# Induced attention and two MLPs: chunk 1's softmax steps, a PSUM bank, a sign vector and four dummy products are moved or added

## The chip, the cores and the metric

The kernel runs on one core of a Trainium2 chip. Its time is the device time of one execution in microseconds (us); the time before is the median of three runs, 992.58 us (991.95 to 992.87). The engines are named as the profile names them: PE is TensorE's products, PEld its weight loads, DVE is VectorE, ACT is ScalarE, POOL is GpSimd, SP is SyncE, which here issues transfers. A q behind a name is the engine's instruction queue.

## The reference

There are 12480 tokens x of 128 channels and 32 inducing vectors. Then come three stages, one after the other, all in float32 (the MLP weights arrive as float64):

```python
def mab(q, kv):
    s = scale * (q @ kv.transpose(0, 2, 1))
    s = s - s.max(-1, keepdims=True)
    a = np.exp(s)
    a /= a.sum(-1, keepdims=True) + 1e-09
    return a @ kv
h = mab(I, x)              # 32 rows
x = mab(x, h)              # 12480 rows
h = x @ w_in;  x = (h * np.cos(h)) @ w_out             # 128 -> 2048 -> 128
h = x @ w_in2; out = (h / (1 + np.exp(-h))) @ w_out2   # 128 -> 2048 -> 128
```

## The kernel before, in words

**Prologue (lines 284 to 688, up to about 50 us).** The tokens are loaded and transposed, and the first attention is done over all of them. Its result is folded into the first MLP's input weights (`project`, 628 to 648). `project_hi` on ScalarE and `project_lo` on VectorE write the stacked weights `hw[0..3]`; `project_lo` reads the sign vector `s_w`, which lies in the prologue's pool `pp` (line 294). The softmax of chunk 0 is done here too, and `spread(1)` issues the sixteen transfers that put block 1's weights of attention into the stack buffer `stk`.

**Main loop (`main`, 716 to 1005).** Tokens go through in 7 chunks (lines 70 to 74): chunk 0 has 8 tiles, chunk 6 has 10, the others 16. Each chunk makes 4 blocks of up to 512 columns, chunk 0 makes 2, so there are 26 blocks. A block takes 8 steps, one for each pair of hidden tiles of 128, so there are 208 steps (NU), and the second MLP runs L2 = 11 steps behind the first. The code emits the instructions of a step in a fixed order by hand (969 to 1005), and each engine takes its own in that order:

- `mlp1_in(s)` (727): two products into `h1` (two buffers in PSUM); `mlp1_act` (742): Sin on ScalarE, the multiply on VectorE, the rounded copy `hi`; `mlp1_rest` (788): the remainder `lo` on VectorE; `mlp1_out` (823): six products into `acc1`, in steps below WHOLE1 = 12 two whole float32 products instead. At the end of a block `y_split` (833) makes `yhi` on ScalarE and `ylo` on VectorE from `acc1`.
- `mlp2_in` (844): six products into `h2` (one buffer); `mlp2_act` (862): Silu and `hi` on ScalarE, `lo` on GpSimd; `mlp2_out` (887): six products into `acc2` two steps later (below WHOLE2 = 8 two whole ones); `store` (897) at the end of a block: a transpose on VectorE and transfers.
- `held_back` (963 to 967) tells where in a step `mlp2_in` and Silu stand: 0 is ahead of `mlp2_out`, 1 behind it, 2 behind `mlp1_out` too.
- `joined`, `worded` and `splitting` (704 to 708) tell in which early steps the remaining weight pieces are converted: `narrow_body` and `narrow_tail` on ScalarE, `narrow_sign` and the first half of `narrow_join` on VectorE, its sum on GpSimd, followed by the transfer of a further piece (`fetch`) on SP's queue; `split` is a cast on ScalarE and a subtraction on GpSimd. Step 4 begins with the body of the piece that step 0 fetched.

**Softmax of the later chunks.** `soften` (928) does one of six things: take (scores by products into the bank of `h2`, transposed by VectorE at line 220), centre (a maximum on VectorE, a subtraction on GpSimd), exp (ScalarE, with a table load before and after), norm (230: sum, add and reciprocal on VectorE, the multiply on GpSimd), turn (237: a transpose on VectorE), split (240: a cast on ScalarE, a subtraction on GpSimd). `chunk_step` (944) looks up which thing a chunk does in which step: `second` (710) for chunk 1, by step; `later` (711) for the others, counted from 24 steps ahead of the chunk's first block, which is a multiple of 8. `attend` (949) calls them, exp early in a step, the rest at its end behind the weight split. `fill` (956) issues a block's transfers into the stack; block 2, the first of chunk 1, is needed by the products of step 16 and was filled at the end of step 15.

**PSUM.** It has eight banks: h1 takes 0 to 3, h2 takes 4 and 5, acc1 is 6 and acc2 is 7. Projections 2 and 3 lie in banks 4 and 5 in the prologue, projections 0 and 1 in 6 and 7.

Of the kernel before, what the change touches and what calls it, by code (L numbers as in the profile page):

```python
# [9 lines left out]
F32 = mybir.dt.float32  # L10
# [11 lines left out]
def tile_induced_attention_then_two_mlps(  # L22
# [31 lines left out]
    nc = tc.nc  # L54
# [4 lines left out]
    P, G, Q = 128, 4, 32  # L59
    NF = FF // P  # L60
    NJ = NF // 2
# [19 lines left out]
    persist = ctx.enter_context(tc.tile_pool(name="persist", bufs=1))  # L81

    half_pi = persist.tile([P, 1], F32, name="half_pi")
    quarter = persist.tile([P, 1], F32, name="quarter")
    hT4 = persist.tile([C, G, M], F32, name="hT4")

    held = persist.tile([P, G * W], F32, name="held")
# [4 lines left out]
    hw = [persist.tile([P, FF // 4], F32R, name=f"hw{i}") for i in range(4)]  # L92
# [152 lines left out]
    blocks, first_of = [], []  # L245
# [11 lines left out]
    stacks = {}  # L257

    def places(b):

        at, out = 0, []
        for g, t, m in blocks[b][1]:
            n = width((t, m), g)
            out.append((g, t, m, at, n))
            at += n
        return out

    def cols(b):
        return sum(n for *_, n in places(b))

    def spread(b, st):
        t0 = st["span"][0]
        stack = stk[:, b % 2, :]
        for g, t, m, at, n in places(b):
            a = (t - t0) * Q
            for r in range(G):
                src = st["hi"].bitcast(F32) if r < 2 else st["lo"]
                nc.sync.dma_start(
                    out=stack[r * Q : (r + 1) * Q, at : at + n].bitcast(F32),
                    in_=src[g * Q : (g + 1) * Q, a : a + n],  # L280
                )
        stacks[b] = stack

    with ExitStack() as pro:
        pp = pro.enter_context(tc.tile_pool(name="pp", bufs=1))
# [5 lines left out]

        fold = pp.tile([P, M], F32, name="fold")
        fold4 = pp.tile([P, G, M], F32, name="fold4")
        s_w = pp.tile([P, 1], F32, name="s_w")
        ones = pp.tile([P, 1], F32, name="ones")
        warm = pp.tile([P, 1], F32, name="warm")
        indT = pp.tile([C, M], F32, name="indT")
# [25 lines left out]
        spin = ps_h.tile([P, 512], F32, tag="hp", name="spin")[:, 0:P]  # L323
# [220 lines left out]
        for i in range(end):  # L544

            k = i - 2 if i < 2 + NP else None
# [51 lines left out]
            lhsT=fold4.rearrange("p g m -> p (g m)"),  # L598
            rhs=zacc[end % 2],
            start=True,  # L600
            stop=True,
# [3 lines left out]
        spin = ps_h.tile([P, 512], F32, tag="hp", name="spin")[:, 0:P]  # L605
# [65 lines left out]
        for i, v in enumerate((hi0, lo0)):  # L671
            for g, t, m, at, n in places(0):
                nc.tensor.matmul(
                    top[:, at : at + n],
                    lhsT=pick[:, g, 2 - 2 * i : 6 - 2 * i, :].rearrange("p r m -> p (r m)"),
                    rhs=v[:, t * Q : t * Q + n],
                    start=(i == 0 and g == 0),
                    stop=(i == 1 and g == G - 1),
# [13 lines left out]
    psh = ctx.enter_context(tc.tile_pool(name="psh", bufs=1, space=PSUM, reuse_waits="tile"))  # L692
    psa = ctx.enter_context(tc.tile_pool(name="psa", bufs=1, space=PSUM, reuse_waits="tile"))
# [6 lines left out]
    LEAD, FILL = 24, 8  # L700
# [6 lines left out]
    splitting.update(zip((13, 15, 11, 12), range(NP, 2 * NP)))  # L707
    splitting.update(zip((17, 18, 19, 20), range(3 * NP, 4 * NP)))

    second = {3: "take", 5: "centre", 12: "exp", 13: "norm", 14: "turn", 14.5: "split"}  # L710
    later = {0: "take", 2: "centre", 5: "exp", 7: "norm", 10: "turn", 11: "split"}

    def d1(u):
        return 2 if u < WHOLE1 else 1
# [1 line left out]
    def main(general):  # L716
# [3 lines left out]
        acc1, acc2 = {}, {}  # L720
# [6 lines left out]
        def mlp1_in(u):  # L727
            b, j = divmod(u, NJ)
            n = cols(b)
            ps = psh.tile([P, 2, 512], F32, tag="h1", name="h1", bufs=2)  # L730
            for a in range(2):
                f = 2 * j + a
                nc.tensor.matmul(  # L733
                    ps[:, a, 0:n],
                    lhsT=hw[f // 4][:, f % 4 * P : (f % 4 + 1) * P],
                    rhs=stacks[b][:, 0:n],
                    start=True,
                    stop=True,
                )
            hid1[u] = ps  # L740

        def mlp1_act(u):
            b, j = divmod(u, NJ)
            n = cols(b)
            h = hid1.pop(u)[:, :, 0:n]
            whole = u < WHOLE1
            c = u1.tile(
                [P, 2, W],
                F32,
                tag=("hi1", "lo1")[u % 2] if whole else "c",  # L750
                name="c",
                bufs=2 if whole else 1,
            )
            cs = c[:, :, 0:n]
            if general:
                turns = cs.bitcast(I32)
                nc.scalar.activation(turns, h, AF.Identity, bias=quarter, scale=0.5 / PI)
                nc.vector.scalar_tensor_tensor(
                    out=cs,
                    in0=turns,  # L760
                    scalar=2.0 * PI,
                    in1=h,
                    op0=ALU.mult,
                    op1=ALU.subtract,
                )
                nc.scalar.activation(cs, cs, AF.Sin, bias=half_pi, scale=-1.0)
            else:
                nc.scalar.activation(cs, h, AF.Sin, bias=half_pi, scale=1.0)  # L768
            if u in worded:
                narrow_body(worded[u])  # L770
                narrow_tail(worded[u])

            nc.vector.tensor_tensor(cs if whole else h, h, cs, ALU.mult)  # L773
            if whole:
                g1[u] = c
                join(u)
                return
            hi = u1.tile([P, 2, W], F32R, tag="hi1", name="hi1")
            nc.vector.tensor_copy(hi[:, :, 0:n], h)  # L779
            join(u)  # L780
            g1[u] = (hi, h)
# [31 lines left out]
        def down_whole(acc, w, c, j, n):  # L813
            for a in range(2):
                nc.tensor.matmul(  # L815
                    acc[:, 0:n],
                    lhsT=w[:, 2 * j + a, :],
                    rhs=c[:, a, 0:n],
                    start=(j == 0 and a == 0),
                    stop=(j == NJ - 1 and a == 1),  # L820
                )

        def mlp1_out(u):
            b, j = divmod(u, NJ)
            n = cols(b)
            if j == 0:
                acc1[b] = psa.tile([P, 512], F32, tag="acc1", name="acc1")
            if u < WHOLE1:
                down_whole(acc1[b], wf1, g1.pop(u), j, n)
            else:  # L830
                down(acc1[b], wo1, g1.pop(u), j, n)
# [112 lines left out]
        def chunk_step(k, s):  # L944
            if k == 1:
                return second.get(s)
            return later.get(s + LEAD - first_of[k] * NJ)

        def attend(s, early):
            for k in range(1, NK):  # L950
                for at in (s, s + 0.5):
                    what = chunk_step(k, at)
                    if what and (what == "exp") == early:
                        soften(chunk_soft[k], what)

        def fill(s):
            for b in range(2, NB):
                if s == b * NJ - (1 if b == 2 else 5 if blocks[b][0] == 1 else FILL):
                    spread(b, chunk_soft[blocks[b][0]])

        held_back = {}
        for k in range(1, NK):
            for s in range(NU):
                if chunk_step(k, s) == "exp":
                    held_back[s + 1], held_back[s + 2] = 2, 1

        for s in range(NU + L2 + D2 + 1):
            if s < NU:  # L970
                mlp1_in(s)
            v = s - L2
            place = held_back.get(s, 0)
            into = [False] * 3
            if 0 <= v < NU:
                into[place] = True
            if into[0]:
                mlp2_in(v)
            if s < L2:
                out1(s)  # L980
            if s < NU:
                mlp1_act(s)
            attend(s, True)
            if into[0]:
                mlp2_act(v)
            v = s - L2 - D2
            if 0 <= v < NU:
                mlp2_out(v)
                if v % NJ == NJ - 1:
                    store(v // NJ)  # L990
            v = s - L2
            if into[1]:
                mlp2_in(v)
                mlp2_act(v)
            if s < NU:
                mlp1_rest(s)
            if s >= L2:
                out1(s)
            if into[2]:
                mlp2_in(v)  # L1000
                mlp2_act(v)
            if s in splitting:
                split(splitting[s])
            attend(s, False)
            fill(s)

    hot = nc.values_load(flag[0:1, 0:1], min_val=0, max_val=1)
    saved = dict(stacks)
    ahead = len(order) - len(pieces)
    with tc.If(hot == 0) as arm:  # L1010
        main(False)
    stacks = saved
    with arm.Else():
        main(True)
# [34 lines left out]
```

## Time and profile before

| | us |
|---|---|
| median of three runs | 992.58 |
| the profiled execution's own time | 992.66 |
| its span, first to last instruction | 990.8 |
| prologue, up to the first product of the main loop | 48.8 |
| steps 0 to 16, up to the products of step 17 | 48.8 to 114.6 |
| a plain step later on | 4.59 |

How to read it: the rows come from one execution, so lengths are compared within it, and a gain is made against its 992.66 us. A product's own duration overlaps with the next one's, so the pace is read from starts. An idle stretch in brackets is the engine's idle time just before that row, with what ended it. PEclk is the granted share of TensorE's full clock of 2.4 GHz; its other level is 1.2 GHz, which is 0.5.

### The profile page before, as it was taken

Reading aid. Unit: us, or ns where it says so; the run is one execution under the profiler, and the core shown is the slowest. Engines: PE = TensorE matmul, PEld = TensorE weight load, DVE = VectorE, ACT = ScalarE, POOL = GpSimd, SP = SyncE. Lnnn points to the kernel's source line nnn. Section 1 sums busy time; section 2 is a strip of 40 time slices with the busy share of each in tenths; the row PEclk is TensorE's granted clock in tenths of the full one; section 3 lists DMA queues with packets and bytes.
Section 4 is the critical chain, followed back from the end, with each engine's and each line's share of the span. In section 5 each row is a group of like instructions: output and inputs, shape, how many; then the busy total and the mean of one; then the engine's idle time right before and its main releaser. Section 6 shows DMA issues by size and latency. Waiting matters only on the chain.

```text
span 990.8 us, 12394 instructions
## 1 busy us (share of the span) xinstructions
PE 966.6 (98%) x4659; PEld 773.5 (78%) x4659; DVE 786.5 (79%) x818; ACT 703.1 (71%) x764; POOL 507.9 (51%) x265
## 2 busy tenths in 40 slices
PE   8889899999999999999999999999999999999997
PEld 6545577788887788887788887788887888889996
DVE  4877778888888888888888888888888888867871
ACT  5777466876776777776877676867766867777774
POOL 1244255555545554555554555555555555465555
PEclk9989899999999999999999999999999999999999
DMA  9331010010110100110100100100100100000000
GB/s 350 105 118 40 22 22 1 11 30 3 22 22 1 22 16 7 22 19 3 23 12 10 22 16 6 22 12 11 22 13 9 22 11 8 18 17 13 13 8 16
DMA packets 65229, 28.21 MB, mean 28 GB/s; under 512 B 54312, under 2 KB 59784, under 8 KB 65160
## 3 DMA queue, kind: packets, MB, share of 16 engines
q1 hardware_dynamic: 64504, 27.24, 11.1%
q8 instruction: 38, 0.62, 0.3%
q14 instruction: 31, 0.25, 0.1%
q10 hardware_dynamic: 656, 0.09, 0.1%
HBM read 14.79 MB, written 6.39 MB: 21 GB/s over the span
## 4 chain that ended last, share of the span: by engine, by line
PE 80%; DVE 9%; ACT 3%; issue 2%; POOL 1%; DMA 0%; SPq 0%; ACTq 0%; POOLq 0%
PE acc L805 46%; PE h L853 24%; PE h L733 8%; DVE lo L795 2%; DVE h L773 2%; DVE hi L779 2%; ACT c L768 2%; PE acc L815 1%; ACT s L868 1%; DVE ylo L839 1%; POOL tail L152 0%; DVE sm L232 0%; DVE sm L233 0%; DVE s L220 0%; DVE sign L144 0%
## 5 line engine op out<-in xcount | busy, mean ns | idle before, releaser
L877 POOL TENSOR_TENSOR lo<-s,hi 128x1024 fp32r<-128x1024 f32 (+2 forms) x197 | 448.0, 2274 | 387.0 <-ACT hi L876 355.8
L805 PE MATMUL acc<-hi,wo 128*128 128x512 f32 (+2 forms) x1584 | 409.7, 380 | 0.9 <-DVE ylo L839 0.7
L773 DVE TENSOR_TENSOR h<-h,c 128x1024 f32<-128x1024 f32 (+2 forms) x196 | 227.5, 1161 | 136.6 <-ACT c L768 136.2
L805 PEld LDWEIGHTS acc<-hi,wo 128*128 128x128 f32 x1584 | 288.2, 188 | 60.2 <-DVE ylo L839 3.0
L768 ACT ACTIVATE c<-h,half_pi 128x1024 f32<-128x1024 f32 (+2 forms) x208 | 221.2, 1064 | 157.6 <-PE h L733 155.7
L868 ACT ACTIVATE s<-h 128x1024 f32<-128x1024 f32 (+2 forms) x208 | 202.5, 974 | 73.1 <-PE h L853 69.8
L853 PE MATMUL h<-yhi,wi 128*128 128x512 f32 (+2 forms) x832 | 248.8, 381 | 2.9 <-DVE s L220 2.2
L805 PE MATMUL acc<-lo,wo 128*128 128x512 f32 (+2 forms) x792 | 235.3, 378 | 0.1
L779 DVE CAST hi<-h 128x1024 fp32r<-128x1024 f32 (+2 forms) x196 | 226.1, 1154 | 6.8
L795 DVE TENSOR_TENSOR lo<-h,hi 128x1024 fp32r<-128x1024 f32 (+2 forms) x196 | 225.1, 1149 | 5.8
L876 ACT CAST hi<-s 128x1024 fp32r<-128x1024 f32 (+2 forms) x197 | 196.8, 999 | 6.3
L853 PEld LDWEIGHTS h<-yhi,wi 128*128 128x128 f32 x832 | 152.3, 188 | 36.4 <-DVE s L220 4.4
L805 PEld LDWEIGHTS acc<-lo,wo 128*128 128x128 f32 x792 | 145.8, 188 | 29.6 <-POOL lo L882 0.4
L853 PE MATMUL h<-ylo,wi 128*128 128x512 f32 (+2 forms) x416 | 157.4, 378 | 0.0
L733 PE MATMUL h<-stk,hw 128*128 128x512 f32 (+2 forms) x416 | 128.2, 389 | 8.0 <-DMA stk<-at 4.0
L733 PEld LDWEIGHTS h<-stk,hw 128*128 128x128 f32 x416 | 76.4, 190 | 33.7 <-issue 12.1
L853 PEld LDWEIGHTS h<-ylo,wi 128*128 128x128 f32 x416 | 78.4, 188 | 14.6
L815 PE MATMUL acc<-c,wf 128*128 128x512 f32 x48 | 24.3, 632 | 1.4 <-DVE ylo L839 1.4
L838 ACT CAST yhi<-acc 128x512 fp32r<-128x512 f32 (+2 forms) x26 | 14.6, 560 | 15.1 <-PE acc L805 14.9
L900 DVE STREAM_TRANSPOSE o<-acc 128x512 f32<-128x512 f32 (+2 forms) x26 | 17.5, 674 | 7.6 <-PE acc L805 7.6
L839 DVE TENSOR_TENSOR ylo<-acc,yhi 128x512 fp32r<-128x512 f32 (+2 forms) x26 | 16.9, 649 | 7.7 <-ACT yhi L838 7.7
L773 DVE TENSOR_TENSOR c<-h,c 128x1024 f32<-128x1024 f32 x12 | 14.7, 1222 | 7.3 <-ACT c L768 5.9
(141 smaller groups left out, 330.3 us busy)
## 6 DMA issues: line engine op xcount, KB each, us to landing
out_dram<-o SPq DMA_DIRECT2D x80, 64.0 KB, 2.0
x_sb<-in_x_dram SPq DMA_DIRECT2D x8, 512.0 KB, 9.9
raw<-in_moe_w_in_dram SPq DMA_DIRECT2D x8, 512.0 KB, 5.4
raw<-in_moe_w_out_dram SPq DMA_DIRECT2D x8, 512.0 KB, 3.8
stk<-ahi SPq DMA_DIRECT2D x40, 64.0 KB, 2.0
stk<-at SPq DMA_DIRECT2D x40, 64.0 KB, 2.0
x_sb<-in_x_dram SPq DMA_DIRECT2D x3, 256.0 KB, 3.3
x_sb<-in_x_dram SPq DMA_DIRECT2D x2, 320.0 KB
```

The source lines that it names most:

```text
L733: nc.tensor.matmul(ps[:, a, 0:n], lhsT=hw[f // 4][:, f % 4 * P : (f % 4 + 1) * P], rhs=stacks[b][:, 0:n], start=True, stop=True,)
L768: nc.scalar.activation(cs, h, AF.Sin, bias=half_pi, scale=1.0)
L773: nc.vector.tensor_tensor(cs if whole else h, h, cs, ALU.mult)
L779: nc.vector.tensor_copy(hi[:, :, 0:n], h)
L795: nc.vector.tensor_tensor(lo[:, :, 0:n], h, hi[:, :, 0:n].bitcast(F32), ALU.subtract)
L805: nc.tensor.matmul(acc[:, 0:n], lhsT=wt[:, 2 * j + a, :], rhs=gt[:, a, 0:n], start=(j == 0 and p == 0 and a == 0), stop=(j == NJ - 1 and p ...
L815: nc.tensor.matmul(acc[:, 0:n], lhsT=w[:, 2 * j + a, :], rhs=c[:, a, 0:n], start=(j == 0 and a == 0), stop=(j == NJ - 1 and a == 1),)
L839: nc.vector.tensor_tensor(lo[:, 0:n], y[:, 0:n], hi[:, 0:n].bitcast(F32), ALU.subtract)
L853: nc.tensor.matmul(ps[:, a, 0:n], lhsT=wt[:, fs], rhs=yt[:, 0:n], start=(p == 0), stop=(p == 2),)
L868: nc.scalar.activation(sv, hid2.pop(u)[:, :, 0:n], AF.Silu)
L876: nc.scalar.copy(hv, sv)
L877: nc.gpsimd.tensor_tensor(lv, sv, hv.bitcast(F32), ALU.subtract)
```

## The change

`s_w` is put into the lasting pool, behind `half_pi` and `quarter`, so it outlives the prologue. Chunk 1 does norm and turn at the end of step 12 (as 12.25 and 12.5) and split at the end of step 13; they stood in steps 13, 14 and 14. The transfers of block 2 are issued in step 13 instead of 15. The other chunks do exp and norm one step sooner. `acc1` of block 0 takes the bank of `acc2`. In the step after a take, `mlp2_in` and Silu stand behind `mlp2_out`. In step 1, four products with 512 columns that nobody reads are issued into the bank of `h2`.

```diff
     quarter = persist.tile([P, 1], F32, name="quarter")
+    s_w = persist.tile([P, 1], F32, name="s_w")
...
-        s_w = pp.tile([P, 1], F32, name="s_w")
...
-    second = {3: "take", 5: "centre", 12: "exp", 13: "norm", 14: "turn", 14.5: "split"}
-    later = {0: "take", 2: "centre", 5: "exp", 7: "norm", 10: "turn", 11: "split"}
+    second = {3: "take", 5: "centre", 12: "exp", 12.25: "norm", 12.5: "turn", 13: "split"}
+    later = {0: "take", 2: "centre", 4: "exp", 6: "norm", 10: "turn", 11: "split"}
...
+        def keep_awake(n):
+
+            ps = psh.tile([P, 2, 512], F32, tag="h2", name="spin")
+            for _ in range(n):
+                nc.tensor.matmul(
+                    ps[:, 0, :], lhsT=hw[0][:, 0:P], rhs=stacks[0], start=True, stop=True
+                )
...
-                acc1[b] = psa.tile([P, 512], F32, tag="acc1", name="acc1")
+                acc1[b] = psa.tile([P, 512], F32, tag="acc1" if b else "acc2", name="acc1")
...
-                for at in (s, s + 0.5):
+                for at in (s, s + 0.25, s + 0.5):
...
-                if s == b * NJ - (1 if b == 2 else 5 if blocks[b][0] == 1 else FILL):
+                if s == b * NJ - (3 if b == 2 else 5 if blocks[b][0] == 1 else FILL):
...
                 if chunk_step(k, s) == "exp":
                     held_back[s + 1], held_back[s + 2] = 2, 1
+                elif chunk_step(k, s) == "take":
+                    held_back[s + 1] = 1
...
                 mlp1_in(s)
+            if s == 1:
+                keep_awake(4)
```

## Rows read from the trace of the kernel before

**Rows 1.** The page, part 1: busy time, share of the span, instructions.
```profile
PE 966.6 (98%) x4659; PEld 773.5 (78%) x4659; DVE 786.5 (79%) x818; ACT 703.1 (71%) x764; POOL 507.9 (51%) x265
```
**Rows 2.** Timeline of PE, 48 to 110: start, length, work, [idle before].
```profile
53.16 1.22 PE L733 MATMUL h<-stk,hw 128*128 128x512 f32 x2 [3.13 <-DVE c L773]
...
76.33 1.98 PE L815 MATMUL acc<-c,wf 128*128 128x512 f32 x4 [1.35 <-DVE ylo L839]
...
106.94 1.19 PE L733 MATMUL h<-stk,hw 128*128 128x512 f32 x2 [4.04 <-DMA stk<-at]
```
**Rows 3.** Windows of early stages: stretch, length, busy by engine, PEclk, DMA share, GB/s.
```profile
53.20:57.70 4.50, 4.50 (x7) 2.24 (x8) 3.57 (x6) 3.46 (x5) 2.05 (x2) 0.52 0.10 26
...
75.00:90.00 15.00, 13.13 (x39) 7.20 (x40) 10.01 (x11) 13.35 (x18) 6.36 (x5) 1.00 0.19 50
...
107.00:113.00 6.00, 6.00 (x13) 3.76 (x13) 5.17 (x5) 3.28 (x4) 2.52 (x2) 0.57 0.18 44
```
**Rows 4.** Windows of single steps: after take, plain, behind norm and the y split.
```profile
303.20:308.62 5.42, 5.00 (x25) 3.78 (x21) 4.53 (x5) 3.20 (x3) 1.31 (x2) 1.00 0.02 3
308.62:313.21 4.59, 4.59 (x21) 3.75 (x20) 2.96 (x4) 3.19 (x3) 2.40 (x2) 1.00 0.00 0
340.80:345.84 5.04, 4.86 (x22) 3.68 (x20) 4.94 (x6) 3.68 (x4) 3.45 (x3) 1.00 0.00 0
```
**Rows 5.** Table of waits: who waited for whom, us, times, longest.
```profile
PEld h L853 <- DVE s L220: 4.4, 5, 1.0
...
PEld acc L805 <- DVE ylo L839: 3.0, 5, 0.6
```
**Rows 6.** Timeline of all engines, 42 to 66.
```profile
47.74 2.70 DVE L641 SCALAR_TENSOR_TENSOR hw<-hw,s_w,hwps 128x512 fp32r<-128x512 f32 x4
...
48.83 1.20 PE L733 MATMUL h<-stk,hw 128*128 128x512 f32 x4 [0.74 <-ACT stk L680]
...
50.68 1.11 ACT L768 ACTIVATE c<-h,half_pi 128x1024 f32<-128x1024 f32 x1 [1.91 <-DVE hw L641]
...
58.40 1.30 SPq L128 DMA_DIRECT2D raw<-in_moe_w_in_dram  x3
...
62.64 0.67 ACT L135 ACTIVATE body<-raw 128x512 f32<-128x512 f32 x1
```
**Rows 7.** The page, part 6: issues, KB each, median us to landing.
```profile
raw<-in_moe_w_out_dram SPq DMA_DIRECT2D x8, 512.0 KB, 3.8
```
**Rows 8.** Timeline of DVE, 84 to 110 and 321 to 323.
```profile
91.32 1.23 DVE L773 TENSOR_TENSOR h<-h,c 128x1024 f32<-128x1024 f32 x1 [3.18 <-ACT c L768]
...
94.79 1.22 DVE L795 TENSOR_TENSOR lo<-h,hi 128x1024 fp32r<-128x1024 f32 x1
...
96.64 0.98 DVE L233 TENSOR_SCALAR sm<-sm 128x16 f32<-128x16 f32 x1
...
101.46 0.70 DVE L238 STREAM_TRANSPOSE at<-s 128x512 f32<-128x512 f32 x1
...
322.02 0.71 DVE L900 STREAM_TRANSPOSE o<-acc 128x512 f32<-128x512 f32 x1
```
**Rows 9.** Timeline of ACT, 84 to 110.
```profile
102.20 0.62 ACT L241 CAST ahi<-at 128x512 fp32r<-128x512 f32 x1 [4.62 <-DVE at L238]
```
**Rows 10.** Timeline of POOL, 84 to 108.
```profile
90.35 1.29 POOL L179 TENSOR_TENSOR wo<-wf,wo 128x512 fp32r<-128x512 f32 x1 [3.44 <-ACT wo L178]
...
97.98 1.05 POOL L235 TENSOR_TENSOR s<-s,sm 128x512 f32<-128x512 f32 x1 [0.40 <-DVE sm L234]
...
102.89 1.26 POOL L242 TENSOR_TENSOR at<-at,ahi 128x512 f32<-128x512 f32 x1 [3.86 <-ACT ahi L241]
```
**Rows 11.** The chain that ended last, 84 to 125: start, length, work.
```profile
104.73 2.07 DMA stk<-at
...
114.61 0.47 PE h L733 x2
...
119.59 0.47 PE h L733 x2
```

## The prediction

> **What bounds the kernel now.** I read the page's engine shares first, then the timeline and the windows of the stages in which TensorE idles, then the length of single steps and the table of waits. TensorE is busy 98% of the span [rows 1], so only time in which it stands, or runs at the lower of its two clock levels (1.2 and 2.4 GHz), can be won. Before 115 us chains of the other engines bind: the products stand 3.13, 1.35 and 4.04 us [rows 2], and the granted clock is 0.52 after the first stand and 0.57 after the last [rows 3]. After 115 us a plain step takes 4.59 us, and two steps of a chunk are longer for a wait: the one after "take" (5.42) and the one behind "norm" and the y split (5.04) [rows 4]. There are five such chunks [rows 5].
>
> The profiled execution took 992.66 us, 0.08 above the median of 992.58. The sum is made against 992.66.
>
> **The first wait (s_w, dummy products, bank).** Sin of step 0 starts at 50.68, held by project_lo, which ends at 47.74 + 2.70 = 50.44 [rows 6]. The tile c of step 0 lies over the prologue's pool, and what project_lo reads there is s_w. Once s_w has its own place, Sin(0) waits for its products alone; they start at 48.83 [rows 6], so by about 49.6 they are done, 1.1 us sooner. The multiply behind it, and with it the products that start at 53.16 [rows 2], then come near 52.0. Should another tile hold Sin(0) as well, this gain is nil, and the sum hardly moves, as follows.
>
> The four dummy products write the bank pair of h2, where projections 2 and 3 are read until 50.44. So they run from 50.5, at 4.59 / 20 = 0.23 each [rows 4] or, at the low clock, twice that, and end between 51.4 and 52.3: 0 to 0.3 us at the third step's products. Whatever clock they keep, Sin(4), at 61.6 now, comes sooner by 1 to 2.9 us. There the gain stops: the next piece on ScalarE is "body", now at 62.64, which reads a weight piece issued at 58.40 [rows 6], behind sixteen stack transfers on SP's queue, and that issue doesn't move. A piece of these weights takes a median of 3.8 us to land where it goes alone [rows 7], so body starts at 62.2 at the earliest. Between 0 and 0.44; I take **0.4**, since what precedes body gains more than that in every case.
>
> From body to step 12 a loop sets the time: Sin, multiply, sign, GpSimd's join, ScalarE's split, next Sin. The stand of 1.35 on ylo [rows 2] is what the other bank for block 0's acc1 removes. The loop doesn't pass through it; the products would stand for the next multiply instead. Taken at **0**, bounds 0 and 1.35.
>
> **Second chunk.** Now the turn comes at 101.46, in step 14, behind that step's VectorE pieces and step 13's norm [rows 8]. ScalarE stands 4.62 us for it, up to 102.20, in front of Sin(15) [rows 9]. Then follow GpSimd's subtraction (to 104.15 [rows 10]), the transfers (to 106.80 [rows 11]) and the products of step 16 at 106.94 [rows 2]. The change moves norm (three small VectorE pieces, one GpSimd multiply) and turn to the end of step 12, the split and block 2's four transfers to the end of step 13; SP's queue has nothing else in those steps.
>
> - The exponential keeps its place on ScalarE, ahead of the cast that GpSimd waits for at 90.35 [rows 10]. VectorE is idle from 88.14 (91.32 less 3.18 [rows 8]); norm's three pieces took 1.9 us (96.01 to the multiply at 97.98 [rows 8, 10]) and fit there.
> - The multiply is queued on GpSimd behind that weight split, which ends at 91.64; 1.05 more is 92.7 [rows 10]. This is the wait that the change adds: VectorE stands on the turn until 92.7, and Sin(13)'s multiply behind it, now at 91.32, goes at 93.4. Step 13's pieces come 2.1 us later, its lo at 98.1 instead of 96.0 [rows 8].
> - Steps 14 and 15 get it back: norm (1.9) and turn (0.70 [rows 8]) no longer stand in them, and Sin(15) waits for no turn. lo(14) ends near 101.8 (now 101.5). The products of step 13's output end 0.8 later, those of step 14's near 103.5 (now 106.94 - 4.04 = 102.9 [rows 2]).
> - The stack: GpSimd takes step 13's join (from 97.0, when its sign piece is ready), a weight split and then the subtraction, three of about 1.28 [rows 10]: 100.85. From that piece's end to the landing it took 106.80 - 104.15 = 2.65: 103.5. The products of step 16 start at about 103.55 with next to no stand.
> - That is 106.94 - 103.55 = 3.4 us, and the clock doesn't fall: step 16's products, at the low clock, take 114.61 - 106.94 = 7.67, the next step's, of the same number, 119.59 - 114.61 = 4.98 [rows 2, 11]; 2.6 more. Together **6.0**; bounds 0.9 (rival b) and 7.
>
> From step 17 on products bound each step as before; VectorE's 3.7 us of pieces, 4.8 with a weight join, are inside 4.98.
>
> **After take.** The second MLP's products stand until VectorE's transpose has freed h2, and the step takes 5.42 instead of 4.59 [rows 4], five times [rows 5]. Put behind six output products (6 x 0.23 = 1.4 us), whose operands were ready a step before, they find it free. Silu comes 0.5 us later, for which ScalarE (3.20 busy of 5.42 [rows 4]) has room. 5 x 0.83 = **4.15**; bounds 0 and 4.15.
>
> **exp and norm a step sooner.** The step at 340.80 takes 5.04 [rows 4] because the y split stands on VectorE behind what norm has left over [rows 5]. In one step more VectorE makes up about 0.9 (4.59 less 3.7), over the 0.45. What is late next: exp now shares its step with the store, and in the next step the first product of the new acc2 comes right behind two h products. The store's transpose ends at 322.73 [rows 8]; those h products run from 308.62 + 3 x 4.59 = 322.39 [rows 4] to 322.85. It fits by 0.1. 5 x 0.45 = **2.25**; bounds -1 (0.2 late each time) and 2.25. Loads of ScalarE's table stay at two per chunk.
>
> **Sum**: 0.4 + 0 + 6.0 + 4.15 + 2.25 = 12.8, and 992.66 - 12.8 = **979.9**.
>
> **Rivals.**
> (a) *The clock falls again in the first stage.* The products now run ahead of the loop and stand often, for short times. For: it was low after the stand of 3.13. Against: in 75 to 90 they were busy 13.13 of 15 us, with the stand of 1.35, and the clock stayed at 1.00 [rows 2, 3]. A fall costs what it cost in step 16, 2.6 to 2.7: 982.6. The Trainium skill (TensorE: Matmul & The Clock Gate, section "A second HAM failure mode: psum-queue depth-cycling") says that frequent short idling between groups of products makes the clock swing between its levels. By that rule this rival would hold; the row of 75 to 90 does not agree with it.
>
> (b) *The stack is late after all.* VectorE's stand on the turn pushes step 13's join, and the join and a split go ahead of the subtraction on GpSimd. With two pieces of 1.28 more in front, or VectorE's small pieces stretched as the add of 0.98 is beside a GpSimd piece [rows 8], the stack lands at 106; the products stand 2.5 us and the clock falls: step 17 at 113.7, a gain of 0.9 for 6.0: 985.0.
>
> (c) *The first stage carries its gain through.* If body's piece lands well before 62.2, Sin(4) at 58.7 pulls the loop along: 2.5 more, 977.4. Against: the issue at 58.40 and its 3.8 us [rows 6, 7].
>
> (d) *Slower.* s_w is declared ahead of nearly every lasting tile, so stack, weights and unit buffers all move in SBUF. If pieces read more slowly at the new places, each step pays. It decides from 12.8 / 190 steps = 67 ns a step, 3.4 ns a product of 230; at 100 ns a step it is 979.9 + 19 = 999. For: nothing in the rows. Against: the twenty products of a step read many tiles at many places and keep one pace [rows 4].
>
> **How the numbers follow.** Forecast 0.68, (a) 0.11, (b) 0.09, (c) 0.07, (d) 0.05. The time is the likeliest's, 979.9. The range runs from 976.5, a little below (c), to 985.0, the time of (b); it leaves out (d) and what lies beyond (b) and (c). A measurement of this kernel tells about 0.2%, 2.0 us, from no change. All but (d) are faster by more than that, and (d) is split between no difference and slower: 0.94, 0.03, 0.03.
>
> **What would show it.** Right: Sin(0) near 49.6; body of step 4 held by its transfer to about 62.2; the norm multiply right behind a weight split near 91.6, with VectorE idle in front of the turn; step 16's products between 103.2 and 103.6, not held by the stack; no low clock between 60 and 960; 4.6 us for the step after take and for the one behind norm. Wrong: a wait on the store in the step after exp, a stand of over 1 us for the stack, or a pace other than 4.59 in plain steps.

## The result and the profile after

The changed kernel takes 980.74 us (median of four runs, 979.62 to 981.40), the kernel before 992.27 in the four runs beside it: a ratio of 0.9884, with a 95% interval of 0.9867 to 0.9901. The profiled execution of the changed kernel took 980.35 us, 12.31 less than the profiled one of before.

The engine shares, columns as in [rows 1]:
```profile
PE 961.5 (98%) x4663; PEld 771.0 (79%) x4663; DVE 785.2 (80%) x818; ACT 701.7 (72%) x764; POOL 507.7 (52%) x265
```
TensorE is busy 5.1 us less, though it has four products more. The rest of the gain is time in which it stood. The timeline of PE, 46 to 112, against [rows 2]:
```profile
48.25 1.18 PE L733 MATMUL h<-stk,hw 128*128 128x512 f32 x4 [0.73 <-ACT stk L680]
...
49.93 1.19 PE L746 MATMUL spin<-stk,hw 128*128 128x512 f32 x4 [0.50 <-DVE hw L641]
51.62 0.74 PE L733 MATMUL h<-stk,hw 128*128 128x512 f32 x2 [0.50 <-DVE c L781]
...
76.75 0.74 PE L733 MATMUL h<-stk,hw 128*128 128x512 f32 x2 [1.18 <-DVE c L781]
...
96.91 0.73 PE L813 MATMUL acc<-lo,wo 128*128 128x512 f32 x2 [0.60 <-DVE lo L803]
...
102.43 0.63 PE L733 MATMUL h<-stk,hw 128*128 128x512 f32 x2
...
107.40 0.63 PE L733 MATMUL h<-stk,hw 128*128 128x512 f32 x2
```
The stand of 3.13 is now two of 0.50 with the dummy products (`spin`) between them, and the one of 4.04 on the stack is gone: the products of step 16 start at 102.43 with no idle time ahead of them, those of step 17 follow 4.97 later. The stand of 1.35 on ylo is now one of 1.18 on a multiply. New is one of 0.60 on a lo piece.

Windows of the same stages, against [rows 3], then of four single steps: after take, plain, after exp, behind the y split, against [rows 4]:
```profile
51.60:57.20 5.60, 5.58 (x21) 2.27 (x21) 4.65 (x7) 4.21 (x6) 2.55 (x2) 1.00 0.10 25
...
75.00:90.00 15.00, 13.12 (x41) 7.39 (x40) 10.49 (x14) 13.34 (x17) 6.15 (x6) 1.00 0.12 36
...
107.00:113.00 6.00, 6.00 (x24) 4.23 (x23) 5.90 (x8) 3.13 (x4) 0.00 (x0) 1.00 0.01 1
...
295.10:299.84 4.74, 4.74 (x25) 3.86 (x21) 3.85 (x5) 2.23 (x3) 1.04 (x1) 1.00 0.00 0
299.84:304.43 4.59, 4.59 (x21) 3.75 (x20) 3.43 (x4) 4.06 (x4) 2.67 (x2) 1.00 0.00 0
...
313.62:318.35 4.73, 4.73 (x22) 3.68 (x20) 2.57 (x3) 3.52 (x4) 2.06 (x1) 1.00 0.32 55
...
332.14:336.73 4.59, 4.59 (x21) 3.75 (x20) 4.52 (x5) 3.68 (x4) 2.41 (x2) 1.00 0.00 0
```
The granted clock (last column but two) is 1.00, the level of 2.4 GHz, where it had been 0.52 and 0.57. The step after take is 4.74 instead of 5.42, the one behind the y split 4.59 instead of 5.04; the step after exp is 4.73, where a plain one takes 4.59.

The first product of the main loop came at 48.83 before and 48.25 now, and between 47.74 and 49.04 in the profiles of all the kernels here. Kernels whose edits don't touch the prologue spread over it (47.92 to 49.04), so it is the prologue's own scatter, and stages are compared from this product on. Two marks serve below: "first split" is ScalarE's first cast of a weight piece (wi) behind the body of step 4, 14.96 us after the first product before and 14.43 now; "step 17" is that step's first product, at 65.62 before and 59.15 now. The marks scatter too: in the changed kernel and the experiments that leave all this as it is, the first split lies at 14.42 to 14.65 and step 17 at 59.15 to 59.37. A difference of 0.2 us in one of them shows nothing. Where 12.31 us went:

| | gain, us | forecast |
|---|---|---|
| prologue, scatter | 0.58 | - |
| first wait, up to the first split | 0.53 | 0.4 |
| from there to step 17 (second chunk) | 5.94 | 6.0 |
| five steps after take | 3.48 | 4.15 |
| five steps behind the y split | 2.20 | 2.25 |
| five steps after exp | -0.60 | 0 |
| sum | 12.13 | 12.8 |

Nearly all of the 0.18 that is left lies in the five steps behind the long ones, which took 4.60 to 4.63 before and take 4.59 now.

### The profile page after: what moved, and what is told of

It reads as the page before. It is cut to its first block, busy times and chain, and to the rows that moved or that the text cites. A ratio compares the mean times of both kernels' runs of the same rounds, so it can differ in the third digit from the quotient of the medians.

```text
span 978.5 us, 12403 instructions
## 1 busy us (share of the span) xinstructions
PE 961.5 (98%) x4663; PEld 771.0 (79%) x4663; DVE 785.2 (80%) x818; ACT 701.7 (72%) x764; POOL 507.7 (52%) x265
## 4 chain that ended last, share of the span: by engine, by line
PE 93%; DVE 2%; ACT 1%; POOL 1%; issue 1%; SPq 1%; DMA 0%; POOLq 0%; ACTq 0%
PE acc L813 52%; PE h L862 27%; PE h L733 8%; PE pt L369 1%; PE acc L823 1%; SPq L279 1%; PE hp L517 1%; PE s L402 1%; DVE sign L145 1%; ACT c L776 1%; PE s L199 1%; POOL tail L153 1%; PE spin L325 0%; DVE sign L142 0%; ACT s L877 0%
## 5 line engine op out<-in xcount | busy, mean ns | idle before, releaser
L733 PE MATMUL h<-stk,hw 128*128 128x512 f32 (+2 forms) x416 | 125.3, 382 | 3.9 <-DVE c L781 3.0
L847 ACT CAST yhi<-acc 128x512 fp32r<-128x512 f32 (+2 forms) x26 | 14.6, 560 | 13.6 <-PE acc L813 13.4
```

The source lines that it names most:

```text
L733: nc.tensor.matmul(ps[:, a, 0:n], lhsT=hw[f // 4][:, f % 4 * P : (f % 4 + 1) * P], rhs=stacks[b][:, 0:n], start=True, stop=True,)
```

## The experiments

Each is an edit of the changed kernel; diffs run from it to the experiment.

**The second chunk, undone.**
```diff
-    second = {3: "take", 5: "centre", 12: "exp", 12.25: "norm", 12.5: "turn", 13: "split"}
+    second = {3: "take", 5: "centre", 12: "exp", 13: "norm", 14: "turn", 14.5: "split"}
...
-                if s == b * NJ - (3 if b == 2 else 5 if blocks[b][0] == 1 else FILL):
+                if s == b * NJ - (1 if b == 2 else 5 if blocks[b][0] == 1 else FILL):
```


> The changed kernel, with chunk 1's steps and block 2's transfers back where they stood before (norm 13, turn 14, split 14.5, transfers in step 15). Theory (the second chunk's stall and the low clock behind it are 6 us): TensorE stands about 4 us for the stack ahead of step 16, the granted clock falls to 0.5 around there, step 17's products come at about 113.5 instead of 107.4, time 986.7. Rival (the clock was kept up by the dummy products and the earlier first stage, so that only the stand returns): no low clock near 105 to 112, step 17 at 110.8, time 984.1.

Measured: 987.23 us, 0.9949 of before (0.9932 to 0.9965). Step 17 came 65.06 after the first product, 5.9 later than in the changed kernel. PE's timeline and a window of this experiment:
```profile
105.80 1.19 PE L733 MATMUL h<-stk,hw 128*128 128x512 f32 x2 [3.97 <-DMA stk<-at]
```
```profile
107.00:113.00 6.00, 6.00 (x15) 3.73 (x15) 4.16 (x4) 3.28 (x4) 2.02 (x2) 0.65 0.09 22
```
The stand on the stack is back, and the clock is 0.65 in the window behind it. There the products are busy all the time and only 15 are recorded, where 24 are in the changed kernel's. Step 16's products start 3.3 us later than in the changed kernel, and from there to step 17 it takes 7.6 us instead of 5.0. So the 5.9 us are the stand and the clock together, as the theory had it. The first stage's gain is kept beside the late stack: step 17 comes 0.56 sooner than in the kernel before (65.62).

**The step after take, undone.**
```diff
-                elif chunk_step(k, s) == "take":
-                    held_back[s + 1] = 1
```


> The changed kernel without the new order in the step after take. Theory (that order alone made the step after take shorter): the five steps after take go from 4.74 back to about 5.42, 0.68 each, nothing else moves: 984.1. Rival (the shorter step comes from exp and norm having moved, so that VectorE is free sooner for the transpose): the steps stay at 4.7, time 980.7.

Measured: 984.95 us, 0.9926 (0.9910 to 0.9943). The five steps take 5.38 to 5.50 again, with the wait on VectorE's transpose:
```profile
297.04 0.73 PE L862 MATMUL h<-yhi,wi 128*128 128x512 f32 x2 [0.42 <-DVE s L221]
```
These products start 1.15 us after the h products of their step (295.89); in the changed kernel the products in that place follow after 0.57. From this pair to the next product it takes 0.57, in the changed kernel 0.47. Together that is about the 0.67 by which the step is longer. The rival is out.

**exp and norm of the later chunks: both back, norm alone, exp alone.** Each differs in the dictionary `later` (the changed kernel's line stands first).
```diff
-    later = {0: "take", 2: "centre", 4: "exp", 6: "norm", 10: "turn", 11: "split"}
+    later = {0: "take", 2: "centre", 5: "exp", 7: "norm", 10: "turn", 11: "split"}
```


> The changed kernel with exp and norm of the later chunks back at 5 and 7. Theory: the five steps behind the y split go from 4.59 back to 5.04, and the step after exp, 4.69 to 4.73 in the changed kernel, back to 4.60: +2.2 less 0.6, time 982.3. Rival (the step after exp is long because of its held-back order and not because the store's transpose shares the step): it stays at 4.7 when exp moves, +2.2, time 982.9.

Measured: 982.09 us, 0.9895 (0.9878 to 0.9911). The steps behind the y split take 5.00 to 5.04, those after exp 4.60:
```profile
332.23:337.27 5.04, 4.86 (x21) 3.68 (x20) 4.94 (x6) 3.68 (x4) 3.44 (x3) 1.00 0.00 0
```
Both sides of the exchange came back. The rival is out: the step after exp has the same held-back order wherever exp stands, and here it is not long.

```diff
+    later = {0: "take", 2: "centre", 5: "exp", 6: "norm", 10: "turn", 11: "split"}
```


> The changed kernel with exp of the later chunks back at 5 and norm left at 6. Theory (the gain behind the y split is norm's, the 0.1 us in the step after exp is the store's transpose): the steps behind the y split stay at 4.59, and the steps after exp are 4.60 again: 0.6 us faster than the changed kernel, 980.1. Rival (norm one step after exp finds exp not done, VectorE stands on its sum, and its late pieces lengthen a step): one step per chunk is longer by 0.5 or more, time 983.

Measured: 985.30 us, 0.9926 (0.9909 to 0.9942). The theory was wrong. The rival's reason was wrong too: VectorE doesn't stand in front of the sum. Two steps of each chunk are long, 4.84 to 4.88 and 5.19; a window of the first, VectorE's timeline and GpSimd's:
```profile
327.87:332.74 4.87, 4.86 (x22) 3.64 (x20) 4.77 (x6) 3.98 (x4) 3.71 (x3) 1.00 0.00 0
```
```profile
326.62 1.56 DVE L234 TENSOR_SCALAR sm<-sm 128x16 f32<-128x16 f32 x1
```
```profile
325.76 2.40 POOL L886 TENSOR_TENSOR lo<-s,hi 128x1024 fp32r<-128x1024 f32 x1 [2.03 <-issue]
```
The add of 1e-9 on 16 elements a partition takes 1.56 us (in chunk 6, on 10 elements, 1.93) and ends at 328.18, within 0.02 of the end of GpSimd's piece, 325.76 + 2.40 = 328.16. In the changed kernel the add of the five later chunks takes 0.36 to 0.56, with exp alone moved (below) 0.17. To see whether this was all, the add was left out:
```diff
+    later = {0: "take", 2: "centre", 5: "exp", 6: "norm", 10: "turn", 11: "split"}
...
-        nc.vector.tensor_scalar_add(sm, sm, 1e-9)
```


> The changed kernel with exp of the later chunks back at 5, norm left at 6, and without the addition of 1e-9 to the sums of the second attention (the sums are at least 1, where float32 doesn't see it). With the addition this kernel's steps 32 and 33 took 4.87 and 5.19, and the add took 1.57 us in step 30, up to the end of a GpSimd piece. Theory (VectorE's small add waits for GpSimd's piece to end, and this is what makes the y split late): without it the sum and the reciprocal take 0.7 and 0.25, step 32 is 4.6 and step 33 at most 4.75, time 981. Rival (any small VectorE piece in that place waits so): the reciprocal takes over 1 us instead, steps 32 and 33 stay long, time 985.

Measured: 980.25 us, 0.9874 (0.9857 to 0.9892); this kernel lacks the 1e-9 in the sums of the second attention. Its VectorE, its GpSimd and the step's window:
```profile
325.71 0.68 DVE L233 TENSOR_REDUCE sm<-s 128x16 f32<-128x512 f32 x1
326.42 0.25 DVE L234 RECIPROCAL sm<-sm 128x16 f32<-128x16 f32 x1
```
```profile
325.55 2.41 POOL L885 TENSOR_TENSOR lo<-s,hi 128x1024 fp32r<-128x1024 f32 x1 [2.03 <-issue]
```
```profile
327.66:332.26 4.60, 4.60 (x22) 3.75 (x20) 4.50 (x5) 4.06 (x4) 3.96 (x4) 1.00 0.01 1
```
The sum and the reciprocal keep their 0.68 and 0.25 although both run while GpSimd's piece does, and the two long steps take 4.59 to 4.60. So the add's wait was the loss of the kernel above, 985.30 against 980.25. The rival is out. The Trainium skill (SBUF — State Buffer, section "Who interferes with whom") says that a tensor_scalar may need the pair of SBUF ports that VectorE shares with GpSimd, that it then waits until GpSimd's instruction gives them up, and that a tensor_reduce on this chip never does. The rows agree: the add ends with GpSimd's piece, the sum (0.67 there, 0.68 here) isn't stretched.

```diff
+    later = {0: "take", 2: "centre", 4: "exp", 7: "norm", 10: "turn", 11: "split"}
```


> The changed kernel with exp of the later chunks at 4 and norm back at 7. Theory (exp, which holds ScalarE for its two table loads and makes VectorE 2.6 us late, is what has to be further from the y split; norm alone leaves VectorE 1 to 2 us late, which it makes up): the steps behind the y split stay at 4.59 to 4.65, the steps after exp at 4.70, time 980.7 to 981. Rival (norm next to the y split is the cause, as the prediction had it): the steps behind the y split are 5.0 again, time 983.

Measured: 981.04 us, 0.9889 (0.9872 to 0.9907). Windows of the step after exp and of the one behind the y split:
```profile
314.50:319.20 4.70, 4.70 (x22) 3.67 (x20) 2.55 (x3) 3.51 (x4) 2.03 (x1) 1.00 0.32 56
333.00:337.60 4.60, 4.60 (x22) 3.75 (x21) 4.53 (x5) 3.68 (x4) 2.42 (x2) 1.00 0.00 0
```
With norm in its old step, right ahead of the y split, the step behind the split is as short as a plain one: exp's earlier place alone brings the 0.45, and the rival, that norm's place by itself makes the step long, is out. It is not the only way. The kernel without the add has exp in its old place and norm one step sooner, and there the step is short too. So the split is late where VectorE has both to work off in too few steps, what exp has held up and norm's pieces. With both moves undone, its `ylo` starts 2.80 us into the step; with exp alone moved 1.67, with norm alone moved and no add 1.63. How exp holds VectorE up is read from its timeline in the changed kernel, behind exp:
```profile
317.21 1.23 DVE L781 TENSOR_TENSOR h<-h,c 128x1024 f32<-128x1024 f32 x1 [2.16 <-ACT c L776]
...
321.76 1.23 DVE L781 TENSOR_TENSOR h<-h,c 128x1024 f32<-128x1024 f32 x1 [0.80 <-ACT c L776]
```
VectorE stands 2.16 us for a Sin that exp has held up on ScalarE, and in the step after only 0.80; behind that it doesn't stand until the y split is done. One step more between exp and the y split gives it the time to come back.

**The first stage: all three parts undone, the dummies alone undone.** The first of the two moves `s_w` back into `pp`, gives block 0's acc1 its own bank and drops the dummy products; the second is the last lines alone:
```diff
-            if s == 1:
-                keep_awake(4)
```


> The changed kernel with the sign vector back in the prologue's pool, block 0's sum back in its own bank and no dummy products. Theory (the first stage's gain is cut off by the weight piece that step 4's body waits for): the clock falls to 0.5 near 50 again and the products stand 3 us, Sin of step 4 comes 2.5 to 3 us later from the start of the main loop on, body stops waiting for its transfer, and step 17 comes only 0.5 later: time 981.3. Rival (the gain is carried through): step 17 comes 2 to 3 us later, time 983.2.

> The changed kernel without the four dummy products alone. Theory (the dummies only fill a wait whose end and whose clock do not set the time): the products idle about 1.8 us ahead of step 2 and the clock may fall to 0.5 behind it, yet body of step 4 still starts with its transfer near 61.5, step 17 at 107.4, time 980.7. Rival (the dummies are what keeps the first stage short): with the low clock Sin of step 4 comes after the weight piece has landed, step 17 comes 1 us or more later, time 981.7 or more.

Measured: 981.43 us, 0.9892 (0.9875 to 0.9908), and 981.09, 0.9884 (0.9870 to 0.9900). Such small differences are read from the marks. Step 17 came at 59.65 and 59.38, against 59.15 to 59.37 where nothing of the first stage is changed, the first split at 14.88 and 14.58, against 14.42 to 14.65. All three parts together are worth 0.3 to 0.5 us; the dummies alone are worth nothing that shows above the scatter. PE's timeline without the three parts:
```profile
52.17 1.22 PE L733 MATMUL h<-stk,hw 128*128 128x512 f32 x2 [3.14 <-DVE c L781]
...
75.26 1.98 PE L823 MATMUL acc<-c,wf 128*128 128x512 f32 x4 [1.33 <-DVE ylo L848]
```
Both old stands are back, 4.5 us together, and the loop is later by no more than those 0.3 to 0.5 us. ScalarE's timeline of the same kernel:
```profile
60.00 1.11 ACT L776 ACTIVATE c<-h,half_pi 128x1024 f32<-128x1024 f32 x1 [1.07 <-PE h L733]
61.12 0.67 ACT L135 ACTIVATE body<-raw 128x512 f32<-128x512 f32 x1
```
Here Sin runs up to the body, which doesn't wait for its transfer. In the changed kernel Sin is done long before and the transfer holds the body:
```profile
61.54 0.69 ACT L136 ACTIVATE body<-raw 128x512 f32<-128x512 f32 x1 [2.16 <-DMA raw<-in_moe_w_in_dram]
62.68 0.60 ACT L179 CAST wi<-tail 128x512 fp32r<-128x512 f32 x1
```
Against the kernel before, Sin(4) gained 2.77 us from the first product on (from 12.80 to 10.03) and 2.16 of it are spent waiting. The landing of this transfer, 3.7 to 3.9 us after its issue, is also where the scatter of the marks comes in: the body starts at 13.28 to 13.52 in the kernels that leave it alone, and the first split comes sooner or later with it.

**The transfers in front of that weight piece.** Eight of the sixteen stack transfers of block 1 were issued in step 2 instead of the prologue, behind the weight piece:
```diff
-    def spread(b, st):
+    def spread(b, st, rows=range(4)):
...
-            for r in range(G):
+            for r in rows:
...
-        lo0 = pp.tile([P, WF], F32R, name="lo0")
+        lo0 = sft["hi"][:, WF : 2 * WF]
...
-        spread(1, first | {"lo": lo0.bitcast(F32)})
+        spread(1, first, (0, 1))
...
+            if s == 2:
+                spread(1, chunk_soft[0] | {"lo": sft["hi"][:, WF : 2 * WF].bitcast(F32)}, (2, 3))
```


> The changed kernel with eight of block 1's sixteen stack transfers (the remainder rows) issued in step 2, behind the weight pieces of steps 0 and 1, on the same queue; their source lies in the unused half of the rounded copy's tile. Theory (the weight piece holds body of step 4, but only 0.5 us further on the loop is held by the join of step 3 on GpSimd, as it is in the kernel before): body starts near 59.3 without a wait for its transfer, the first weight split of the main loop comes 0.5 sooner counted from the first product of the main loop (13.9 instead of 14.43), and step 17 comes 0.5 sooner (58.65 instead of 59.15 from that product on): 980.2. Rival (the transfer alone is what holds the loop): both come about 2 us sooner, 978.7.

Measured: 980.37 us, 0.9881 (0.9864 to 0.9897); step 17 at 58.69, 0.46 sooner than in the changed kernel, and the first split at 13.91; both lie below the scatter. ScalarE's timeline:
```profile
58.78 0.68 ACT L136 ACTIVATE body<-raw 128x512 f32<-128x512 f32 x1
...
61.65 0.62 ACT L179 CAST wi<-tail 128x512 fp32r<-128x512 f32 x1 [1.62 <-POOL tail L153]
```
The body no longer waits and comes 2.25 us sooner after the first product, but the split behind it then waits 1.62 for GpSimd's join. There are two limits some half a microsecond apart, and removing the transfer alone uncovers the second, as the theory had it.

In the other attempt all sixteen went to GpSimd's queue:
```diff
-    def spread(b, st):
+    def spread(b, st, queue=None):
...
-                nc.sync.dma_start(
+                (queue or nc.sync).dma_start(
...
-        spread(1, first | {"lo": lo0.bitcast(F32)})
+        spread(1, first | {"lo": lo0.bitcast(F32)}, nc.gpsimd)
```


> The changed kernel with the sixteen stack transfers of block 1 issued on GpSimd's queue instead of SP's. Theory (the weight piece of step 4's body is late because its transfer is queued on SP behind those sixteen): SP issues the next weight pieces from about 52 on instead of 58, body of step 4 does not wait, starts near 59.4 instead of 61.5, and the loop behind it is pulled along by about 2 us: step 17 at 105.4, time 978.7. Rival (another chain of ScalarE, VectorE and GpSimd is as long): body starts sooner, but step 12 and step 17 gain under 0.5 us, time 980.5. Rival 2 (the transfers take GpSimd's time and its first weight sums come late): slower than the changed kernel.

Measured: 982.28 us, 0.9898 (0.9882 to 0.9915); step 17 at 60.57, 1.4 later: the second rival. GpSimd's timeline:
```profile
46.14 1.18 POOL L279 DMA_DIRECT2D stk<-ahi  x2 [3.20 <-DVE ahi L668]
...
54.17 1.28 POOL L153 TENSOR_TENSOR wf<-sign,tail 128x512 int32<-128x512 int32 x1
```
GpSimd issues for eight microseconds and its first join comes at 54.17 (in the changed kernel at 52.77, with a first product 0.5 us later). ScalarE's next piece stands for that join:
```profile
55.48 0.70 ACT L139 ACTIVATE tail<-raw 128x512 int32<-128x512 uint32 x1 [2.58 <-POOL wf L153]
```
What the body's transfer gains, the late join costs, and more.

**The multiply of chunk 1's norm on VectorE.**
```diff
-                weigh_norm(st, nc.gpsimd)
+                weigh_norm(st, nc.vector if st is chunk_soft[1] else nc.gpsimd)
```


> The changed kernel with chunk 1's norm multiply on VectorE instead of GpSimd. Theory (VectorE stands 3.45 us on the turn for a multiply that is queued behind a weight split, and this makes step 13's lo late by 0.6 us for the products): the stand is gone, the turn starts near 89.3, the products no longer stand 0.60 at 96.9, step 17 comes 0.6 to 0.7 sooner, time 980.1. Rival (what then ends last is the stack or Sin, not VectorE): step 17 stays at 107.4, time 980.7.

Measured: 980.05 us, 0.9871 (0.9855 to 0.9888); step 17 at 58.51, 0.64 sooner than in the changed kernel. From the first split to step 17 it takes 43.92 us, where it is 44.70 to 44.76 in the changed kernel and in those that leave both marks alone. VectorE's timeline of the changed kernel, then of this one:
```profile
91.56 0.71 DVE L239 STREAM_TRANSPOSE at<-s 128x512 f32<-128x512 f32 x1 [3.45 <-POOL s L236]
```
```profile
89.08 0.69 DVE L236 TENSOR_TENSOR s<-s,sm 128x512 f32<-128x512 f32 x1
89.80 0.71 DVE L239 STREAM_TRANSPOSE at<-s 128x512 f32<-128x512 f32 x1
```
Counted from the first product, the turn starts 2.5 us sooner, VectorE doesn't stand in front of it, and TensorE's new stand of 0.60 is gone. That stand was the price of the wait that the change adds on VectorE.

**Both of these together (the last and the one with eight transfers later).**

> The changed kernel with both edits that may shorten it: chunk 1's norm multiply on VectorE, and the eight remainder transfers of block 1 issued in step 2. Theory (two stands on one chain, both gone): step 17 at 58.0 us from the first product of the main loop, against 59.15 for the changed kernel, 1.1 us faster than it: 979.6. Rival (the second is hidden behind the first): 58.5, 980.1.

Measured: 979.21 us (978.81 to 979.88), 0.9868 (0.9852 to 0.9885); step 17 at 57.84. It has the lowest median here. The intervals of the ratios of this kernel and the changed one overlap; the 1.3 us of gain is what the mark at step 17 shows.

## Why the prediction was right, and where it was not

**The time** came within a microsecond, 980.74 for 979.9, inside the range. The terms did not all come as worked out, and 0.58 of the 12.31 is the prologue's scatter, which no term had: without it the profiled gain is 11.73, and this is to be held against the 12.8. (The chances at the end give rival (d) 0.06 in all where its own is 0.05; nothing hangs on it.)

**First wait.** 0.53 for 0.4, by the mechanism given: Sin gains, the body's transfer takes the gain back. Counted from the first product the body was forecast at 62.2 - 48.83 = 13.4 and came at 13.29. That the size came out was in part luck, though. The 3.8 us of [rows 7] are the row of w_out, and body's piece belongs to w_in. Its row in the same part of the page has 5.4, and with that the gain would have been nil:
```profile
raw<-in_moe_w_in_dram SPq DMA_DIRECT2D x8, 512.0 KB, 5.4
```
The piece took 3.7 here (issued at 57.83, body at 61.54); no row shown with the prediction has this for w_in. What the prediction missed is the second limit, GpSimd's join, some 0.5 us behind the transfer. It is why rival (c), 2.5 us from an earlier transfer, could not hold: with the transfer out of the way 0.46 came.

**Bank.** Taken at 0. The stand on ylo went, and one of 1.18 on a multiply took its place, as the prediction said. The bank wasn't undone alone, so its own share isn't shown; it is a part of the 0.3 to 0.5 that all three make.

**Second chunk.** 5.94 for 6.0, step by step: step 16's products come 3.4 us sooner beyond the first wait, as forecast, and from there to step 17 it takes 2.5 us less, for 2.6. (The 7.67 of the prediction sets a start of the chain [rows 11] against one of PE's timeline [rows 2]; on the timeline step 17 started 65.62 us after the first product, step 16 58.11, which is 7.51.) The times forecast stood on the profile of before; less 1.11 (0.58 of prologue, 0.53 of first wait) the multiply was to end at 91.6, the subtraction at 99.7, and step 16's products to start at 102.4. GpSimd's timeline has the first two (and PE's has 102.43 above):
```profile
89.22 1.29 POOL L180 TENSOR_TENSOR wo<-wf,wo 128x512 fp32r<-128x512 f32 x1 [3.45 <-ACT wo L179]
90.47 1.05 POOL L236 TENSOR_TENSOR s<-s,sm 128x512 f32<-128x512 f32 x1
...
98.35 1.29 POOL L243 TENSOR_TENSOR at<-at,ahi 128x512 f32<-128x512 f32 x1
```
The multiply stands right behind the weight split and ends at 91.52, the subtraction at 99.64. Counting each queue the step was moved past (the split on GpSimd, the idle 3 us on VectorE) is what made this term good. Rival (b), a late stack, was out, and the experiment that puts the old places back shows what it would have cost.

**Clock.** Rival (a) was out in this kernel: between 75 and 90 the products were busy 13.12 of 15.00 us, with stands up to 1.18, and the granted clock stayed at 1.00, as it did from 60 to 115 (51.05 of 55.00 busy); what the Trainium skill says of frequent short idling (TensorE: Matmul & The Clock Gate, section "A second HAM failure mode: psum-queue depth-cycling") is not seen in that stretch. The dummies are worth nothing that shows: without them the products before step 2 stood 2.18 us and the clock was 0.50 from 52.0 to 56.6, but until step 12 the loop of the other engines, not the products, sets the time. And they don't always keep the clock up. In the last experiment it was low in spite of them:
```profile
50.60:54.00 3.40, 3.40 (x8) 2.02 (x8) 3.14 (x4) 2.94 (x5) 0.75 (x1) 0.50 0.08 19
```
The stands ahead of this window (0.73 and 0.48) were no longer than those of the changed kernel (0.73 and 0.50). So a fall in the first stage remains possible, but it didn't cost the 2.6 to 2.7 that rival (a) put on it: the first split came at 13.91, as in the kernel with eight transfers later, where the clock stayed at 1.00.

**After take.** 3.48 for 4.15. The step that failed is "5 x 0.83": it took the whole difference between the step and a plain one for the wait. In [rows 4] that step has 5.00 us of busy products to the plain step's 4.59. Of the 0.83 about 0.14 is no wait: the two h products behind the score products run at a slower pace, and still do. From 295.10, right behind the score products, the next product is 0.57 away, in a plain step 0.45 (299.84 to 300.29):
```profile
295.10 0.73 PE L733 MATMUL h<-stk,hw 128*128 128x512 f32 x2
295.67 1.09 PE L813 MATMUL acc<-hi,wo 128*128 128x512 f32 x4
```

**exp and norm.** 2.20 - 0.60 = 1.60 for 2.25. Two steps failed. The first is the reading "the y split stands on VectorE behind what norm has left over", with the price put on it: it named one of two causes, since exp alone gives the whole 2.20 with norm where it was, and it took norm's pieces to be as short in the new place. Moved alone, norm makes the kernel slower than with neither moved (985.30 against 982.09): its add falls beside a GpSimd piece and takes 1.56. Without the add, norm's move is enough. The prediction saw this wait in the 0.98 of [rows 8] and used it for rival (b) alone, not for this term. Its bounds of -1 to 2.25 held only because the change moves exp as well, which puts the add where it takes 0.36 to 0.56. The second is "it fits by 0.1". VectorE's timeline and PE's in the step after exp, with the loads of the weights (PEld):
```profile
313.24 0.71 DVE L909 STREAM_TRANSPOSE o<-acc 128x512 f32<-128x512 f32 x1
```
```profile
313.62 0.62 PE L733 MATMUL h<-stk,hw 128*128 128x512 f32 x2
314.09 1.17 PE L813 MATMUL acc<-hi,wo 128*128 128x512 f32 x4
315.10 0.62 PE L813 MATMUL acc<-lo,wo 128*128 128x512 f32 x2
```
```profile
314.06 0.76 PEld L813 LDWEIGHTS acc<-hi,wo 128*128 128x128 f32 x4 [0.25 <-issue]
```
Next, loads and products of the step after exp with exp and norm back, in the same order but in a step without the store:
```profile
318.66 0.88 PEld L813 LDWEIGHTS acc<-hi,wo 128*128 128x128 f32 x4
```
```profile
318.88 1.08 PE L813 MATMUL acc<-hi,wo 128*128 128x512 f32 x4
319.80 0.62 PE L813 MATMUL acc<-lo,wo 128*128 128x512 f32 x2
```
There the first weights are loaded 0.22 ahead of their product and the four products take 0.92 to the next. With the store in the step the transpose ends at 313.95, the load starts 0.11 behind it and only 0.03 ahead of its product, and the four take 1.01. The prediction counted up to the product; its weights come sooner than that. The order of the products alone is not the cause, as it is the same in both. That the load waits for the transpose fits these times, but the profile doesn't name what released it. The step is 0.10 to 0.14 long in each chunk.

**Slower, rival (d)**, was out: plain steps keep 4.59.

## What to carry over

When a long step is set against a plain one, count its own busy time before calling the difference a wait. Of two steps that are moved together, ask which queue each blocks and what runs beside it in its new place: either move was enough for the y split, norm's only without the add that waits for GpSimd. And where several engines pass work around in a loop, list the limit next in line before pricing the removal of one; here the transfer and the join lay some half a microsecond apart, and 2.8 us of earlier Sin brought about 0.5. And before a gain of a few tenths is put down to a part, see how far the same mark scatters in kernels that don't differ there.

## What was not expected of the hardware

A VectorE add on 16 elements a partition takes 0.17 us in some places and 1.56 in others (1.93 on 10 elements), ending with the GpSimd piece beside it, while beside such a piece a reciprocal of the same size (0.25) and a sum over 512 (0.68) were not stretched; beside work where every step counts, a piece of 0.17 cost some 5 us over the run by where it stood. The granted clock fell to its lower level in one of two kernels whose stands of the products just before were alike, 0.73 and about 0.50. A GpSimd engine that issues transfers is taken for as long: two transfers took 1.18 us of it, and the sixteen kept its first join to 54.17.
